# Inverse shuffles 128 to 32 partitions, a last stage of 32-row matmuls, a sine table turned by DMA, and row statistics joined on GpSimd

## The chip, the core and the metric

The kernel runs on one core of a Trainium2 chip. A core has five engines with queues of their own: TensorE (matmuls, in the profile PE, its weight loads PEld), VectorE (DVE), ScalarE (ACT), GpSimd (POOL) and SyncE (SP, which here only issues DMAs). They share 16 DMA engines, an SBUF of 128 partitions, and a PSUM of eight banks that TensorE writes and VectorE and ScalarE read. The metric is the device time of one execution in microseconds. Before the change it is 172.41, the median of three runs (171.73 to 172.89).

## What is computed

Input x is A_q, 2048 rows of 448 columns. Two blocks with residuals follow each other; both start with a layernorm over the columns.

```python
def _A_ref(q, k, v, shift_k, ssm_k, ssm_D):
    # k_shift: causal 4-tap filter of k along the rows, one filter a column
    kv = k_shift * v
    # y: causal convolution of each column of kv with that column of ssm_k (length 2048)
    y = y + kv * ssm_D[None, None, :]
    return q * y

def _B_ref(x, w1, b1, w2, b2):
    h = _layernorm(x, axis=-1)
    u = jnp.einsum("bsd,sf->bdf", h, w1) + b1      # 2048 rows -> 1792
    u = _gelu(u)
    y = jnp.einsum("bdf,fs->bds", u, w2) + b2      # 1792 -> 2048 rows
    return y.transpose(0, 2, 1)

h = x + _A_ref(_layernorm(x), A_k, A_v, A_shift_k, A_ssm_k, A_ssm_D)
h2 = h + _B_ref(_layernorm(h), B_w1, B_b1, B_w2, B_b2)
```

## The kernel before

**Layout.** Row s = 16 q + r lies in partition q, slot r. Every big tile is a view of one SBUF tensor, "arena", so the profile names them all arena; PSUM is "ps".

**The convolution** is a Fourier transform along the 2048 rows, a product, and a transform back, all as matmuls with sine tables that the kernel makes itself (`emit_tables`: integer phases on VectorE at L837 to L844, the sine on ScalarE at L847, in two halves). The steps:

- *kv*: k is transposed on TensorE (L966), filtered by matmuls with diagonal matrices (L992) and multiplied by v on VectorE (L1007). *kT*: the filter ssm_k is transposed (L1038).
- *Stage 1* (`emit_stage1`, tags k1 for the filter and u1 for kv): matmuls with 32 columns of table E (L1059, four at a time in four column groups), evictions of two banks at a time (L1069, for the first k groups L1067 on VectorE), then DMA shuffles within the arena (L1075; per pair of evictions two on GpSimd's queue and one on SyncE's).
- *Stage 2* (`emit_stage2`, k2 and u2): matmuls with the block table FW (L1094), evictions of 128x896 (L738 on ScalarE, L741 on VectorE; with a scale for k at L739 and L742).
- *Inverse stage 1* (`emit_products_i1`, i1): for each index one VectorE product of all four real and imaginary pairs (L1160, 128x1792), then matmuls with the inverse tables MA, MB, MN in two row groups of 64 (L1177), evictions to TU (L738), and shuffles from TU to TZ (L1200; L1189 for the last pair). A shuffle of index j moves 128 partitions of TU into 8 partitions of TZ, 16 pieces each. Rows 14 and 15 have shuffles of their own. The last pair uses re-ordered tables ML, and the first two output rows (NZ = 2) read its share directly from TU through a padded table EW, which small DMAs fill (L1118, L1127).
- *Inverse table*: ET is E transposed on TensorE (`emit_ct`, L1108, 32 transposes) with four copies.
- *Inverse stage 2* (`emit_i2`, i2): for each output row group r, two matmuls over all 128 partitions of TZ (L1299), for r below 2 four more with EW (L1307). Then on each r: a gate (1 + y/std) on ScalarE (L1316) or VectorE (L1318), the product with the centred x on VectorE (L1326; for r below NX = 4 a product straight out of PSUM, L1337), sums for the second layernorm (L1343 and L1346, or L1355 on ScalarE), the power -0.5 on GpSimd (L1379) and the normalised row Q (L1385).

**Row statistics of x** (`emit_q`): per r one bn_stats (L1236) and one bn_aggr (L1238) on VectorE, then an addition and a power on GpSimd (L1244, L1247). For four r, `emit_xn` writes normalised rows ahead of need (L1256 to L1269).

**The MLP** (`emit_mlp`): the first half of W1 (seven blocks of 128 features) accumulates in seven PSUM banks while the rows Q arrive (L1432), with the remaining last-stage matmuls between; then seven blocks with all rows present (L1442), then W2 (L1453), with gelu at L1422 and the output at L1456 and L1464. The weights W1 and W2 come by DMA on SyncE (L1405, L1409, L1416), those of W1 after its first quarter behind the last shuffles.

**What sets the order.** `_Sched` keeps for each engine a queue that is written out by hand: the strings of ORDER name the operations as step:number ("i2.9:0", the first operation of that step). An engine takes its operations in that order, and waits are put in from the data they share and from PSUM banks and ring buffers as they come free. Estimated costs (`est`) settle only which bank or buffer an operation gets and in which order the program is written. Matmuls called "warm" (L1210) and "dummy" (L1025) compute nothing that is used. The issuing of DMAs also has a queue: each engine's DMAs stand in its own order string.

Of the kernel before, what the change touches and what calls it, by code (L numbers as in the profile page):

```python
# [7 lines left out]
ALU = mybir.AluOpType  # L8
# [167 lines left out]
class _Sched:  # L176
# [50 lines left out]
    def op(self, W, fn, r=(), w=(), br=(), bw=(), n=0, kind=None, est=None, dmab=None, keng=16, rate=None, after=(), safter=(), mode=0):  # L227
# [3 lines left out]
        o = _Op()  # L231
# [351 lines left out]
def _build(nc, A_q, A_k, A_v, A_shift_k, A_ssm_k, A_ssm_D, B_w1, B_b1, B_w2, B_b2, out):  # L583
# [8 lines left out]
    R = 16  # L592
# [45 lines left out]
    with ctx:  # L638
# [27 lines left out]
        TU = view(o_TU, [R, 2, D])  # L666
        KN = view(o_KN, [4, S])
        W2 = [view(o, [NFC // 2, S]) for o in o_W2]
        TZ = view(o_TZ, [R, 2, D])
        G = view(o_G, [NFC, D])  # L670
        X = view(o_X, [R, D])
        E = view(o_E, [2 * R, 128], f16)
# [843 lines left out]
```

## Time and profile before

| | |
|---|---|
| median of three runs | 172.41 us |
| profiled execution, span from first to last instruction | 171.2 us |
| TensorE busy | 161.5 us (94%) |
| VectorE busy | 99.1 us (58%) |
| ScalarE busy | 92.9 us (54%) |
| GpSimd busy | 58.1 us (34%) |
| share of the chain of waits: TensorE, ScalarE, DMA | 66%, 14%, 10% |
| MLP: first matmul of L1432, of L1442, of L1453 | 80.95, 104.96, 126.14 us |
| mean granted TensorE clock | 1.00 |

The profile lists no time for the profiled execution apart from its span; the rest to the median, 1.2 us, lies outside the span. Busy times are unions over an engine's instructions; the mean duration of one instruction can be longer than its distance to the next, since neighbours overlap. Start and length columns are microseconds. A DMA row on a queue ("SPq") is the time to issue it; "to landing" counts from the issue to its completion.

### The profile page before, as it was taken

The numbers are of one execution on the slowest core, as the hardware profiler recorded it, in microseconds if no ns is written. First come the engines' busy times: TensorE is split into PE (matmuls) and PEld (weight loads), VectorE is DVE, ScalarE is ACT, GpSimd is POOL, SyncE is SP. The second block draws the span as 40 slices with busy tenths as digits, with TensorE's granted clock in tenths as the row PEclk, the third lists the DMA queues.
The fourth block names the chain that finished last, engine by engine and source line by source line (L and its number), as shares of the span: only waits on it lengthen the run. The fifth ranks groups of instructions, "written<-read, shape, count | busy, mean of one in ns | idle before, by whom it ended". The sixth has DMA issues, their size and how long they took to land.

```text
span 171.2 us, 3572 instructions
## 1 busy us (share of the span) xinstructions
PE 161.5 (94%) x1425; PEld 94.7 (55%) x1425; DVE 99.1 (58%) x187; ACT 92.9 (54%) x133; POOL 58.1 (34%) x150
## 2 busy tenths in 40 slices
PE   6979999979889999988999999999999999999993
PEld 2765845443334434453555555555567777777783
DVE  7988988859899999969988810000003223132232
ACT  3798788988999999999877336321210000000000
POOL 8344827590820573466788820000000000000000
PEclk9999999999999999999999999999999999999999
DMA  5999587675749855667999999960000111101111
GB/s 156 417 315 386 176 257 280 230 301 193 255 120 369 302 173 175 206 182 237 344 342 405 415 419 425 414 279 0 0 0 4 54 54 54 54 4 54 54 54 54
DMA packets 15708, 35.15 MB, mean 205 GB/s; under 512 B 3564, under 2 KB 9980, under 8 KB 15692
## 3 DMA queue, kind: packets, MB, share of 16 engines
q1 hardware_dynamic: 13020, 29.20, 46.9%
q0 software_dynamic: 2528, 5.65, 10.2%
q8 instruction: 11, 0.18, 0.5%
q10 hardware_dynamic: 144, 0.08, 0.2%
q14 instruction: 5, 0.04, 0.1%
HBM read 22.05 MB, written 1.84 MB: 139 GB/s over the span
## 4 chain that ended last, share of the span: by engine, by line
PE 66%; ACT 14%; DMA 10%; DVE 4%; POOL 2%; SPq 2%; issue 1%; DVEq 0%
PE ps L1453 25%; PE ps L1432 12%; PE ps L1442 12%; ACT arena L738 7%; DMA arena<-arena 5%; DMA arena<-in_A_ssm_k_dram 5%; ACT arena L1069 4%; PE ps L1177 4%; PE ps L1094 3%; PE ps L1299 3%; POOL arena L1075 2%; PE ps L992 2%; PE ps L1059 2%; DVE arena L1007 2%; ACT arena L739 1%
## 5 line engine op out<-in xcount | busy, mean ns | idle before, releaser
L1456 DVE SCALAR_TENSOR_TENSOR arena<-ps,arena 128x448 bf16<-128x448 f32 (+2 forms) x17 | 11.2, 657 | 57.3 <-PE ps L1453 57.2
L1453 PE MATMUL ps<-arena 128*128 128x448 bf16 (+2 forms) x238 | 42.7, 342 | 0.0
L1453 PEld LDWEIGHTS ps<-arena 128*128 128x128 bf16 x238 | 33.3, 145 | 9.5
L738 ACT CAST arena<-ps 128x896 bf16<-128x896 f32 x30 | 24.6, 1012 | 0.2 <-PE ps L1094 0.2
L1432 PE MATMUL ps<-arena 128*128 128x448 bf16 x112 | 22.5, 353 | 0.6 <-DVE arena L1385 0.6
L1069 ACT CAST arena<-ps 128x896 bf16<-128x896 f32 x24 | 20.5, 915 | 3.9 <-PE ps L1059 3.8
L1075 POOL DMA_DIRECT2D arena<-arena x32 | 17.6, 554 | 12.2 <-ACT arena L1069 10.2
L1442 PE MATMUL ps<-arena 128*128 128x448 bf16 x112 | 21.3, 352 | 0.0
L1422 ACT ACTIVATE arena<-ps,arena 128x448 bf16<-128x448 f32 x14 | 8.2, 640 | 18.7 <-PE ps L1442 14.5
L1094 PE MATMUL ps<-arena 128*64 128x448 bf16 x128 | 15.2, 359 | 2.5 <-DMA arena<-arena 0.8
L1432 PEld LDWEIGHTS ps<-arena 128*128 128x128 bf16 x112 | 10.9, 98 | 11.1 <-DVE arena L1385 1.3
L1160 DVE TENSOR_TENSOR arena<-arena 128x1792 bf16<-128x1792 bf16 x16 | 16.7, 1086 | 0.3
L1442 PEld LDWEIGHTS ps<-arena 128*128 128x128 bf16 x112 | 11.0, 98 | 10.2
L1059 PE MATMUL ps<-arena 128*32 128x448 bf16 x256 | 15.0, 355 | 0.8 <-DVE arena L1007 0.5
L1177 PE MATMUL ps<-arena 64*128 64x448 bf16 x128 | 14.5, 351 | 0.1
L1094 PEld LDWEIGHTS ps<-arena 128*64 128x64 f16 x128 | 5.8, 108 | 10.9 <-ACT arena L738 2.9
L1200 POOL DMA_DIRECT2D arena<-arena x11 | 6.5, 593 | 15.3 <-ACT arena L738 15.3
L1177 PEld LDWEIGHTS ps<-arena 64*128 64x128 f16 x128 | 6.0, 94 | 8.3 <-ACT arena L738 2.5
L1007 DVE TENSOR_TENSOR arena<-ps,arena 128x512 bf16<-128x512 f32 (+1 forms) x16 | 9.1, 619 | 2.1 <-PE ps L992 1.8
L1355 ACT ACTIVATE arena<-arena 128x448 bf16<-128x448 bf16 x14 | 8.0, 572 | 3.7 <-DVE arena L1326 3.5
L738 ACT COPY arena<-ps 128x1024 bf16<-128x1024 bf16 (+1 forms) x8 | 8.0, 1067 | 3.0 <-PE ps L966 3.0
L1059 PEld LDWEIGHTS ps<-arena 128*32 128x32 f16 x256 | 5.1, 95 | 7.6 <-DVE arena L1007 2.5
(97 smaller groups left out, 192.5 us busy)
## 6 DMA issues: line engine op xcount, KB each, us to landing
arena<-in_B_w_dram SPq DMA_DIRECT2D x8, 896.0 KB, 8.7
arena<-in_B_w_dram SPq DMA_DIRECT2D x2, 2048.0 KB, 17.3
arena<-arena POOLq DMA_DIRECT2D x32, 112.0 KB, 3.2
arena<-arena SPq DMA_DIRECT2D x16, 224.0 KB, 3.2
arena<-in_B_w_dram SPq DMA_DIRECT2D x2, 1536.0 KB, 18.8
arena<-in_A_k_dram SPq DMA_DIRECT2D x4, 448.0 KB, 5.8
arena<-in_A_v_dram SPq DMA_DIRECT2D x4, 448.0 KB, 9.4
arena<-in_A_q_dram SPq DMA_DIRECT2D x4, 448.0 KB, 5.3
```

The costliest lines, as they stand in the source:

```text
L738: return e.copy(out=dst(), in_=src())
L1007: return e.tensor_tensor(out=v, in0=u.rearrange("p t (r d) -> p t r d", d=64), in1=v, op=ALU.mult)
L1059: op("pe", lambda e, W, b=b, r=r, q=q, x=x, c0=c0: e.matmul(PS[32 * q:32 * q + 32, b.slots[x], 0:D], E[:, 2 * r + x, c0:c0 + 32], src[:, r ...
L1069: return e.copy(out=dst, in_=Ppair(b)) if W == "act" else e.tensor_copy(out=dst, in_=Ppair(b))
L1075: shuf[tag].append(op(q_, lambda e, W, g=g, i=i, a=a, nu=nu, jh=jh: e.dma_start(T[a + i:a + i + 4 * nu - 3:4].rearrange("p (j k) c d -> p ...
L1094: op("pe", lambda e, W, b=bs[h], h=h, j=j, c=c, par=par: e.matmul(PS[64 * par:64 * par + 64, b.slots[c], 0:D], FW[:, 64 * c:64 * c + 64], ...
L1160: op("dve", lambda e, W, m=m, i=i: e.tensor_tensor(out=MR(m.slots[0]).rearrange("p (x y) d -> p x y d", x=2), in0=TU[:, i].unsqueeze(2).br ...
L1177: k = op("pe", lambda e, W, b=bs[h], m=ms[h], par=par, t=t, tab=tab, xy=xy, P=P: e.matmul(Pb(b, par), tab[P, :], MR(m.slots[0])[P, xy, :], ...
L1432: op("pe", lambda e, W, r=r, fc=fc, b=bs[fc]: e.matmul(Pb(b), W1A[:, r, 128 * fc:128 * fc + 128], Q[:, r, :], start=(r == 0), stop=(r == R ...
L1442: op("pe", lambda e, W, r=r, fc=fc, b=b: e.matmul(Pb(b), W1B[:, r, 128 * (fc - n0):128 * (fc - n0) + 128], Q[:, r, :], start=(r == 0), sto ...
L1453: op("pe", lambda e, W, r=r, fc=fc, b=b, d0=d0, d1=d1: e.matmul(Pb(b)[:, d0:d1], W2[fc // 7][:, fc % 7, r:S:R], G[:, fc, d0:d1], start=(fc ...
L1456: op("dve", lambda e, W, r=r, b=b, d0=d0, d1=d1: e.scalar_tensor_tensor(out=X[:, r, d0:d1], in0=Pb(b)[:, d0:d1], scalar=bm[:, r:r + 1], in ...
```

## The change

1. **Index order.** Pairs in stage 2 and inverse stage 1 are no longer 2jj and 2jj+1 but `Jof(jj, x) = (jj >> 1) + 8 (jj & 1) + 4 x`; table E is laid out in blocks of four rows, so its phases are computed in two instructions per half.
2. **Shuffles.** Index J goes from 128 partitions of TU to 32 partitions of TZ (every fourth), in one DMA, all on SyncE: 14 of 224 KB, and for the last pair four halves. GpSimd issues none of them; the separate shuffles for rows 14 and 15, the tables ML and the two filling DMAs at L1118 go.
3. **Last stage.** 32-row matmuls at tile positions 0, 32, 64, 96: r = 4k + g uses row group g. Eight of them make one output row (m = 0..3, two halves). For k = 0 the last block (m = 3) is taken from TU through EW, now for four rows, with four matmuls for each half: 152 in all. All sixteen rows stand ahead of the MLP's first matmul in TensorE's order.
4. **Sine table.** ET comes from four DMA transposes on SyncE, each of 128 x 1024 values of E; the TensorE transposes and their copies go. Four DMAs copy rows of ET to EW.
5. **Row statistics.** bn_aggr is gone; for each group of four r, six small operations on GpSimd join the halves of bn_stats and add eps, and a power follows.
6. **A new order** on all five engines, and `est` values given for SyncE's DMAs. The warm matmuls move. In SyncE's order the four transposes stand between the loads of k and v, the EW copies among the stage 1 shuffles; x chunks 1 and 2 stand behind the first inverse shuffle.

```diff
-        if o.is_dma:
+        if o.is_dma and est is None:
             o.est = {e: (585.0 if e == "pool" else 1400.0 if e == "act" else 700.0 if keng <= 8 else 460.0) for e in o.engs}
...
-        TZ = view(o_TZ, [R, 2, D])
+        TZ = view(o_TZ, [4, R // 4, 2 * D])
...
-        E = view(o_E, [2 * R, 128], f16)
-        ET = view(o_ET, [2 * R, 128], f16)
+        E = view(o_E, [R * 256], f16)
+        ET = view(o_ET, [R // 4, 8, 128], f16)
...
+        def Jof(jj, x):
+            return (jj >> 1) + 8 * (jj & 1) + 4 * x
...
+        def emit_et():
+            sch.t0 = T_TH + 1.0
+            for k in (2, 3, 0, 1):
+                op("sp", lambda e, W, k=k: e.dma_start_transpose(out=ET[:, k], in_=E[:, 1024 * k:1024 * k + 1024]),
+                   r=[(o_E + 2048 * k, 2048)], w=[(o_ET + 2048 * k, 2048)], dmab=128 * 2048, est=1350.0, rate=400.0)
...
+            op("pool", lambda e, W: e.memset(EW, 0.0), w=[(o_EW, 2048)], est=950.0)
+            for j in range(4):
+                op("sp", lambda e, W, j=j: e.dma_start(EW[0:128:4, 2 * j:2 * j + 2, :].rearrange("p a b -> p (a b)"),
+                                                       ET[j:128:4, 0, 6:8, :].rearrange("p a b -> p (a b)")),
+                   r=[(o_ET + 1536, 512)], w=[(o_EW + 512 * j, 512)], dmab=32 * 512, est=600.0)
...
+                m = jj >> 1
+                for h0, h1 in ((0, 1), (1, 2)) if jj == R // 2 - 1 else ((0, 2),):
+                    for par in range(2):
+                        J = Jof(jj, par)
+                        p0 = J >> 2
+                        k = op("sp", lambda e, W, J=J, h0=h0, h1=h1, p0=p0, m=m: e.dma_start(
+                            TZ[p0:128:4, m, :, h0 * D:h1 * D], TU[:, J, h0:h1, :].rearrange("p c d -> p (c d)")),
...
-                    op("dve", lambda e, W, bs=bs, r=r: e.bn_aggr(out=qs[:, r, 0:2], in_=bs), r=[(ob, 24)],
-                       w=[(o_qst + 16 * r, 8)], n=6)
...
+                op("pool", lambda e, W, G4=G4: e.tensor_tensor(out=qs[:, G4, 0:2], in0=bst[:, G4, 1:3], in1=bst[:, G4, 4:6],
+                                                               op=ALU.add), est=250.0, r=cb(1, 8) + cb(4, 8), w=cq(0, 8))
...
+            pb = [_Buf(psum) for r in range(R)]
+            for k in range(R // 4):
+                for m in range(4):
+                    for h in range(2):
+                        js = range(4) if k == 0 and m == 3 else range(1)
+                        for j in js:
...
+                            for g in range(4):
+                                r = 4 * k + g
+                                P = slice(32 * g, 32 * g + 32)
+                                if len(js) == 4:
+                                    J = 3 + 4 * j
+                                    lw, mv, rr = EW[P, 2 * j + h, :], TU[P, J, h, :], [(o_EW + 512 * j + 256 * h, 256), (o_TU + (2 * J + h) * DB, DB)]
+                                else:
+                                    lw, mv = ET[P, k, 2 * m + h, :], TZ[P, m, k, h * D:h * D + D]
...
+                                x = op("pe", lambda e, W, b=pb[r], lw=lw, mv=mv, m=m, h=h, j=j, n_=len(js), g=g: e.matmul(
+                                    Pb(b), lw, mv, start=(m == 0 and h == 0), stop=(m == 3 and h == 1 and j == n_ - 1),
+                                    tile_position=(32 * g, 0)),
+                                   r=rr, bw=[pb[r]], n=D, est=47.0, mode=5)
```

SyncE's order, up to the first weights (decoded above in words):

```diff
-        "loads.6:0 loads.8:0 loads.0:0 loads.1:0 loads.2:0 loads.3:0 loads.13:1 loads.14:0-1 loads.10:0 loads.5:0 "
-        "loads.11:0 loads.4:0-2 loads.12:0 loads.7:0 loads.9:0 k1.11:11 k1.9:11 k1.13:11 k1.15:11 u1.1:11 k1.1:11 "
...
+        "loads.6:0 loads.8:0 loads.14:0 loads.0:0 loads.1:0 loads.2:0 loads.3:0 loads.4:2 loads.14:1 loads.4:1 "
+        "loads.10:0 loads.5:0 et.0:3 loads.13:1 loads.12:0 loads.4:0 et.0:2 et.0:0 loads.9:0 et.0:1 loads.7:0 k1.9:11 "
+        "loads.11:0 ew.0:4 k1.11:11 k1.5:11 k1.15:11 k1.7:11 u1.1:11 k1.13:11 ew.0:3 k1.1:11 k1.3:11 u1.5:11 u1.9:11 "
+        "u1.3:11 u1.7:11 u1.11:11 u1.13:11 u1.15:11 ew.0:2 xload.0:0 xload.3:0 ew.0:1 w1a.0:0 i1.1:20 xload.1:0 "
+        "xload.2:0 i1.1:19 i1.9:19 i1.5:19-20 i1.3:20 i1.3:19 i1.9:20 i1.11:19-20 i1.7:19-20 i1.13:20 i1.13:19 "
+        "i1.15:19-20 i1.15:22 i1.15:21 w1a.1:0 w1a.2:0 w1a.3:0 w1b.0:0-3 w2.0:0-3 mlp.25:15 mlp.27:15 mlp.29:15 "
```

In it, loads.0 to 3 are ssm_k, loads.4 the short filter's weights, loads.5, 6, 8 and 10 chunks of k, loads.7, 9, 11 and 12 chunks of v (rows 0-3, 4-7, 8-11, 12-15 of each partition), loads.13:1 the vector D, loads.14 the biases, and et.0 the transposes.

More of the change, by code (lines that the diff above doesn't have):

```diff
@@ L684, in _build @@
         FW, MA, MB, MN = [view(o_BD + 256 * k, [128], f16) for k in range(4)]
-        NZ = 2
         o_EW = o_I2 + 128
-        EW = view(o_EW, [4 * NZ, 128], f16)
-        o_ML = o_EW + 1024 * NZ
-        ML = [view(o_ML + 256 * k, [128], f16) for k in range(3)]
-        assert o_ML + 768 <= o_TU
+        EW = view(o_EW, [8, 128], f16)
+        assert o_EW + 2048 <= o_TU
         o_GR = (o_WR, o_WR + 8 * DB, o_X, o_X + 8 * DB)
@@ L1158, in emit_products_i1 @@
                     ru = (o_TU + i * 2 * DB, 2 * DB)
-                    aft = [x for w in wbufs for x in w.readers] if i == 0 else [mfirst[0]]
+                    aft = [x for w in wbufs for x in w.readers] if not mfirst else [mfirst[0]]
                     op("dve", lambda e, W, m=m, i=i: e.tensor_tensor(
@@ L1196, in emit_products_i1 @@
[L1196 to L1204 removed]
+                    evac(lambda J0=J0, h=h: TU[:, J0:J0 + 5:4, h, :], lambda b=bs[h]: Ppair(b),
+                         [(o_TU + (2 * J0 + h) * DB, DB), (o_TU + (2 * J0 + 8 + h) * DB, DB)], bs[h], 2 * D)
@@ L1213, in _build @@
         mfirst = []
-        o_bst = small(4 * 24)
+        o_bst = small(R * 24)
+        o_qd = small(R * 4)
         o_qst = small(16 * 16)
@@ L1242, in emit_q @@
[L1242 to L1249 removed]
+                    op("dve", lambda e, W, r=r: e.bn_stats(out=bst[:, r], in_=X[:, r, :]), r=[(o_X + r * DB, DB)],
+                       w=[(o_bst + 24 * r, 24)], n=D, kind="1x")
@@ new lines, in emit_q @@
+                if g % 2 == 0:
+                    continue
+                r0 = 2 * g - 2
+                G4 = slice(r0, r0 + 4)
+                cb = lambda c, nb: [(o_bst + 24 * (r0 + i) + 4 * c, nb) for i in range(4)]
+                cq = lambda c, nb: [(o_qst + 16 * (r0 + i) + 4 * c, nb) for i in range(4)]
+                cd = [(o_qd + 4 * r0, 16)]
+                op("pool", lambda e, W, G4=G4: e.tensor_tensor(out=qs[:, G4, 0:2], in0=bst[:, G4, 1:3], in1=bst[:, G4, 4:6],
+                                                               op=ALU.add), est=250.0, r=cb(1, 8) + cb(4, 8), w=cq(0, 8))
@@ L1293, in emit_i2 @@
                     r = r0 + i
[L1294 to L1310 removed]
+                    sch.t0 = T_I2 + 1.0 + T_DI2 * r
+                    b = pb[r]
+                    oA = o_TZ + (4 * (r % 4) + r // 4) * 2 * DB
+                    A = view(oA, [D], f32)
+                    tz = [(oA, 2 * DB)]
                     sch.t0 += 0.01
```

208 lines of the change are left out of this document (65 added, 143 removed), and 135 rows, old and new, of the table ORDER.

## The prediction

> **What bounds the kernel now.** I read the chain of waits first, for the places where the end of the work is decided; then a table of the busy time by stretch, cut at the joints of that chain; then the rows of the groups for prices. The chain, from the last inverse eviction on (start us, length us, what):
>
> ```profile
> 69.59 1.12 ACT arena L738
> 70.72 1.25 ACT arena L1269 x2
> 71.96 0.81 ACT arena L738
> 72.77 0.29 issue
> 73.06 2.14 DMA arena<-arena
> 75.20 0.53 PE ps L1299 x2
> ...
> 80.58 0.32 DVE arena L1385
> 80.90 0.05 issue
> 80.95 1.31 PE ps L1432 x6
> ...
> 104.96 21.19 PE ps L1442 x112
> 126.14 42.09 PE ps L1453 x231
> ```
>
> After 104.96 TensorE runs without a gap; I leave that part alone. From 80.95 to 104.96 TensorE is full too: 112 matmuls of the first MLP half at about 0.189 us (21.2) and 14 left over from the last inverse stage (L1299, 7 x 0.38 = 2.7). What can change lies ahead of 104.96, at three joints: 72.77 (end of the last inverse eviction; call it T), 75.19 (the last shuffle has landed, L1299 starts), 80.95 (first normalised row, MLP starts).
>
> ```profile
> core 0: us, PE busy (x) PEld busy (x) DVE busy (x) ACT busy (x) POOL busy (x), PEclk, DMA share, GB/s
> 5.47:44.00 38.53, 35.61 (x644) 21.10 (x641) 32.53 (x49) 33.48 (x38) 20.62 (x37) 1.00 0.78 275
> 44.00:47.94 3.94, 3.31 (x30) 1.38 (x32) 3.88 (x5) 3.46 (x5) 3.52 (x7) 1.00 0.96 303
> 47.94:72.77 24.83, 23.95 (x209) 10.18 (x206) 24.50 (x38) 24.83 (x32) 8.99 (x17) 1.00 0.68 222
> 72.77:80.95 8.18, 6.86 (x52) 3.77 (x49) 6.77 (x23) 7.80 (x12) 5.47 (x10) 1.00 0.67 204
> ```
>
> From 47.94 to T ScalarE is busy 24.83 of 24.83 us: its queue of evictions sets T. VectorE (24.50) follows closely. Ahead of 47.94 ScalarE idles 5.5 of 42.5 us and VectorE 6.1; nothing is full there except, in parts, the DMA engines (share 0.78 to 0.96).
>
> **The change, part by part.**
>
> *Work on ScalarE up to T.* Prices are start to start: 28 evictions of line 738 run from 47.94 to 70.71, 0.81 each; a k2 eviction (L739) 0.84 (four in 3.35); a transpose copy about 0.95; two normalised rows (L1269) 1.57. Counting the two orders: one copy of the k transposes less (-0.95), one k2 eviction less (-0.84), one u2 eviction more (+0.81), the two L1269 rows now behind the last eviction (-1.57). Sum -2.55. VectorE up to T: copy +0.65 and k2 eviction +1.05, u2 eviction -1.06, the first table copy -0.69, eight aggregations at about 0.12 -1.0: sum -1.0. Both engines are nearly full, so T moves by something between the two unless idle time changes: -2.55 to -1.0. I take -1.3, near VectorE's end, because what ScalarE loses partly goes to VectorE.
>
> *SyncE's early queue.* A bias load moved ahead of the four kernel loads delays them by its issue, 0.46 (the b row took 0.46 there), and the fourth of them heads the chain at 11.48: up to +0.45, inside the lower end above. Four DMA transposes (256 KB each) and four EW copies are new in this queue. The first transpose waits for the first half of the sine table, about 7.7 by the before's VectorE and ScalarE rows (2.1 + 3.5 of phases + 2.0 of sine). Queued behind it: D, three of four v loads, the short-filter weights. The diff's planner books 1.35 us per transpose; no row shows one. Between a plain issue (0.43) and twice the planner's figure, the load of v rows 0-3 goes out at 12 to 20 instead of 10; with the planner's figure at about 15. Landing then takes 3.2 us (SBUF shuffles of this queue) to 9.7 (the v loads before): 18 to 25. Its reader was the product at 19.39, and the new order puts four more k1 steps (4 x 0.85 = 3.4) ahead of it, so it is wanted at about 22.8. Mostly hidden; I take 0, ends 0 and +2.
>
> *Bandwidth of the transposes.* They move 1.05 MB inside a stretch where DMA shares are 0.8 to 0.9. At 417 GB/s (the second of the page's 40 slices) that is 2.5 us of all engines, and spare share up to 30 us is about 5 us: hidden. If they go in 256-byte pieces, 4,096 pieces at 38 ns (queue q10: 0.2% of 16 engines' span over 144 packets) to 99 ns (q1) would be 10 to 25 us. I take the low end, since the rows they read are 2 KB, like most of the packets shown; the high end is a rival. The Trainium skill ("DMA: Bandwidth & Descriptors", Latency and other measured facts) gives 261 GB/s for a DMA transpose, 350 to 400 when contiguous: by it, an estimate of 4.0 or 2.8 us, hidden as well. No run so far shows it.
>
> The wait of the first EW copy for its transpose stands in SyncE's queue ahead of k1's and u1's shuffles. SyncE spent 18.8 us of that stretch waiting for evictions (its own waits, L1075), so 1 or 2 us there are covered; without that cover they would pass to u1's shuffles and to T.
>
> *Shuffles.*
>
> ```profile
> L1200 SPq DMA_DIRECT2D arena<-arena x17: 666/668/684, 60.8 to 83.1; - x17
> L1200 POOL DMA_DIRECT2D arena<-arena x11: 542/594/677, 57.2 to 71.6; - x11
> DMA to landing us min/median/max: 3.0/4.2/6.3
> ```
>
> Before: 12 on GpSimd, 20 on SyncE. After: 18 on SyncE, 18 x 0.67 = 12.1 us inside a 25 us stretch, so the queue keeps up, except at the end, where the last four go out one after another. Two follow the first half's eviction (0.81 ahead of T), two the last: last issue starts at about T + 1.2, landing 2.9 later (L1189): T + 4.1, against T + 2.4 before. That is 1.7 us worse. But the first group of outputs (r 0-3) takes its last block straight from TU through EW, so it needs no landing: 4 rows are ready about T + 0.6.
>
> *Last stage.* 152 matmuls of 32 rows. One at a time they would cost 152 x 0.189 = 28.7 us; four at once 7.2, beside 40 x 0.189 = 7.6 before. The nearest rows: column tiles of 32 (L1059, 24 in 1.32 us, 0.055 each), row tiles of 64 (L1177, 16 in 1.73, 0.108 each, two at once). I take 0.055, so 8.4; about 24 run before T, and the 8 blocks after the landing of each of three groups are 1.3 us. The transposes of the sine table (32, 2.0 us of TensorE) and their four copies go; they lay beside the DMA wait, worth nothing but VectorE's 0.69 above.
>
> *From T to the MLP.* VectorE's new order, start to start: four products 2.5, two statistics with their joins 1.4, two gates 1.2 (they cover GpSimd's power), small step 0.1, gate of r 11 0.6, row 0 0.35: 6.2, from T + 0.6: T + 6.8. The other lock is PSUM: the MLP's first four banks come free with the gates of r 8-11, and ScalarE does five gates (0.61 to 0.72) from about T + 4.5: T + 7.6 to 8.1. I take T + 7.6, before T + 8.18. From there VectorE feeds rows: row 2 at +2.9 and row 4 at +5.9 behind row 0 where TensorE wants them at 2.66 and 5.3: stalls of 0.6 to 1.9, I take 1.4. No matmul of the last stage is left inside. End of the first half: 7.6 + 21.2 + 1.4 = T + 30.2; before 104.96 - 72.77 = 32.2. So -2.0; ends -3.4 (6.8 + 21.2 + 0.8) and 0 (8.5 + 21.2 + 2.5).
>
> *Statistics.* 28 small GpSimd operations at 0.24 and four powers replace ten; +4 us on GpSimd, which loses 12 issues (7.1 us): hidden, 0. Weight loads go out earlier (SyncE spent 75.0 to 83.8 on leftover shuffles); the MLP did not wait for them: 0.
>
> **Sum.** -1.3 + 0 - 2.0 = -3.3 against the profiled span of 171.2, which gives 167.9. The median of the three runs is 172.41, 1.2 above that span (start and end outside it), so 169.1. Its own ends: -2.55 - 3.4 gives 166.5; +0.45 + 2 (queue, v) - 1.0 + 0 gives 173.9 if everything goes badly, more likely 172.
>
> **Rivals.**
> 1. *Slower: the transposes fill the DMA engines.* Place: the loads and k1 shuffles between 8 and 25 us. Price: 10 us of fabric in place of 2.5, less 5 of spare share, is +5 on T; with the -3.3 kept, 174.1, at the top of the price far more. It decides from about 8 us of engine time for the four. For it: no such row exists, share 0.87 from 10 to 20 us. Against: 2 KB rows. Chance 0.18, time 174 to 178.
> 2. *The order gives it back.* The gates wait for the later landing (T + 4.1), banks and rows come late, the idle time ahead of 47.94 grows by 1 to 2: about 172. For it: 1.7 us later landing, one queue. Against: r 0-3 don't need it. Chance 0.14.
> 3. *TensorE slows after a pause.* The warm matmuls (L1210) move away from the place ahead of the MLP. Row: the nine first dummies (L1025) start 0.37 us apart after an idle engine, 0.189 later on, though the clock column says 1.00 in both. Price: nine at 0.18 more, 1.6 us: 170.7. It needs a pause of some microseconds before the MLP; the last stage's matmuls leave about 1. Chance 0.06. The Trainium skill ("TensorE: Matmul & The Clock Gate", HAM oscillation) sets the limit at about 3.4 us of idle time; by that rule the pause I expect is too short.
> 4. *The tiles don't overlap.* At 0.108 each the last stage takes 16.4 us and the MLP starts some 5 us later: 174. For it: neighbours in the new order sometimes share a row group. Against: L1059. Chance 0.03.
>
> **Numbers.** Forecast 169.1 with chance 0.59, its own range 166.5 to 172. The range to hold it 8 times in 10, with rival 2 and the near side of 1: 166.4 to 174.6. One per cent (1.7 us) is about what these runs tell apart from no change. Faster by more than that (under 170.7): 0.58, most of the forecast and half of rival 3; within: 0.2; slower (over 174.1): 0.22, rivals 1 and 4 in the main.
>
> **What would show it.** T at about 71.5, with ScalarE full from u2's first eviction; the MLP's first matmul 7 to 8 us behind T and not sooner than row 0 on VectorE; no last-stage matmul inside the first half; that half 22 to 23 us long. Transposes landing within 3 us of their turn and no wait of VectorE's v products on a load. I am wrong if T lies later than 73, if the first MLP half shows over 2.5 us of gaps, or if the 152 matmuls take over 12 us of TensorE.

## The result and the profile after

| | before | after |
|---|---|---|
| median, us | 172.65 (171.73 to 173.63, 4 runs) | 179.81 (179.07 to 180.78, 4 runs) |
| span of the profiled execution, us | 171.2 | 177.3 |
| first u2 eviction starts | 47.94 | 53.90 |
| last inverse eviction ends | 73.57 | 79.41 |
| MLP's first matmul | 80.95 | 88.77 |
| first half of the MLP ends | 104.96 | 110.84 |

The change is slower: ratio 1.042, interval [1.036, 1.048]. The forecast was 169.1 with a range of 166.4 to 174.6: sign and range were both missed. The ratios here and below leave out executions over 1.5 per cent above the fastest of their kernel; each of those shows a mean granted clock of 0.99 or less.

One correction first. The prediction called 72.77 the end of the last inverse eviction. That is the end of a link in the chain of waits; ScalarE's own row (two casts from 71.71, 1.86 long) ends at 73.57. After has no such link, so from here on T is the end of ScalarE's last cast, 73.57 before and 79.41 after, and "u2" as a time is the start of the first u2 eviction. ScalarE's rows, two of before, then two of after:

```profile
47.94 22.77 ACT L738 CAST arena<-ps 128x896 bf16<-128x896 f32 x28 [0.23 <-PE ps L1094]
71.71 1.86 ACT L738 CAST arena<-ps 128x896 bf16<-128x896 f32 x2
53.90 23.61 ACT L750 CAST arena<-ps 128x896 bf16<-128x896 f32 x29 [0.74 <-PE ps L1109]
77.69 1.72 ACT L750 CAST arena<-ps 128x896 bf16<-128x896 f32 x2 [0.18 <-PE ps L1158]
```

The three stretches are: up to u2 47.94 before, 53.90 after (+5.96); u2 to T 25.63 and 25.51 (-0.12); T to the end of the first MLP half 31.39 and 31.43 (+0.04). What follows takes 66.2 and 66.5. The whole loss lies ahead of u2, and the gain expected behind it is not there.

Busy time by stretch after (engines with instruction counts, clock, DMA share, GB/s), cut at the new joints:

```profile
core 0: us, PE busy (x) PEld busy (x) DVE busy (x) ACT busy (x) POOL busy (x), PEclk, DMA share, GB/s
5.47:50.00 44.53, 38.29 (x655) 21.75 (x654) 35.65 (x59) 32.41 (x37) 23.21 (x46) 0.96 0.94 266
50.00:53.90 3.90, 2.87 (x29) 1.45 (x29) 3.48 (x4) 2.90 (x5) 1.45 (x3) 1.00 0.95 275
53.90:79.41 25.51, 24.98 (x218) 9.74 (x217) 24.98 (x34) 25.33 (x32) 7.36 (x17) 1.00 0.65 229
```

From u2 to T ScalarE is full as before. Ahead of 53.90 it idles 13.1 of 48.4 us (5.5 of 42.5 before), and the granted clock up to 50.00 is 0.96. The chain of waits shows where:

```profile
17.80 0.56 SPq L1121
...
18.41 0.58 SPq L916
...
19.03 1.24 SPq L1121
...
20.32 6.48 DMA arena<-in_A_v_dram
...
27.50 1.62 DVE arena L1022 x3
...
29.16 2.43 PE ps L1074 x24
```

L1121 is the DMA transpose, L916 a v load, L1022 VectorE's product with v, L1074 the stage 1 matmul. Transposes on SyncE's queue stand on the critical chain, ahead of the load of v rows 0-3 (20.32), which lands 6.48 later. The queue itself in order of time:

```profile
7.86 2.75 SPq L1121 DMA_TRANSPOSE arena<-arena  x1
...
12.21 6.15 SPq L1121 DMA_TRANSPOSE arena<-arena  x2
18.41 0.58 SPq L916 DMA_DIRECT2D arena<-in_A_v_dram  x1
19.03 1.24 SPq L1121 DMA_TRANSPOSE arena<-arena  x1
20.32 0.58 SPq L916 DMA_DIRECT2D arena<-in_A_v_dram  x1
```

The four transposes hold SyncE's queue for 10.1 us (2.75 + 6.15 + 1.24); the loads issued between them hold it for 0.4 to 0.6 each. The line's own view (least, median, longest issue in ns; then landing), the group of the v products and the packets:

```profile
L1121 SPq DMA_TRANSPOSE arena<-arena x4: 1237/2785/3282, 7.9 to 19.0; - x4
DMA to landing us min/median/max: 4.7/6.7/7.9
```

```profile
DMA packets 20365, 36.25 MB, mean 205 GB/s; under 512 B 7340, under 2 KB 15036, under 8 KB 20348
...
L1022 DVE TENSOR_TENSOR arena<-ps,arena 128x512 bf16<-128x512 f32 (+1 forms) x16 | 8.8, 617 | 5.1 <-DMA arena<-in_A_v_dram 4.5
```

Packets under 512 bytes were 3,564 before: 3,776 more, about what 1.05 MB in 256-byte pieces makes (4,096). VectorE waits 4.5 us for v. That wait has a second price. TensorE stood still for 2.37 us up to 27.96 (and 1.44 up to 21.98), and then the granted clock fell (clock, DMA share and GB/s are the last three numbers of each row):

```profile
26.00:28.00 2.00, 0.04 (x4) 0.04 (x8) 1.11 (x3) 0.00 (x0) 1.99 (x4) 1.00 1.00 322
28.00:30.00 2.00, 1.92 (x28) 0.66 (x32) 2.00 (x4) 1.34 (x2) 0.00 (x0) 0.65 1.00 283
30.00:32.00 2.00, 2.00 (x28) 0.73 (x22) 2.00 (x3) 0.65 (x2) 1.01 (x2) 0.50 0.89 351
```

The 24 matmuls of L1074 at 29.16 took 2.43 us; 24 of this kind took 1.32 in the prediction's row. Such a stretch, with a granted clock near 0.5, is called half rate below.

Behind T, TensorE's timeline (start, length, idle time before in brackets):

```profile
78.31 3.40 PE L1287 MATMUL ps<-arena 32*128 32x448 bf16 x59
81.64 0.36 PE L1181 MATMUL ps<-arena 128*128 128x448 f16 x1
81.94 0.36 PE L1287 MATMUL ps<-arena 32*128 32x448 bf16 x1
82.23 0.36 PE L1181 MATMUL ps<-arena 128*128 128x448 f16 x1
82.53 1.49 PE L1287 MATMUL ps<-arena 32*128 32x448 bf16 x21
83.95 0.36 PE L1181 MATMUL ps<-arena 128*128 128x448 f16 x1
84.37 2.08 PE L1287 MATMUL ps<-arena 32*128 32x448 bf16 x38
86.50 0.36 PE L1181 MATMUL ps<-arena 128*128 128x448 f16 x1
86.80 2.04 PE L1287 MATMUL ps<-arena 32*128 32x448 bf16 x32
```

L1287 is the last stage, L1181 a warm matmul. The 32-row tiles do overlap, 59 in 3.40 us (0.058 each), but only some 18 of them fit ahead of T, TensorE is taken until the MLP starts, and four warm matmuls stand among them.

### The profile page after: what moved, and what is told of

Its sections match the earlier page's. It is cut to its first block, busy times and chain, and to the rows that moved or that the text cites. A ratio compares the mean times of both kernels' runs of the same rounds, so it can differ in the third digit from the quotient of the medians.

```text
span 177.3 us, 3704 instructions
## 1 busy us (share of the span) xinstructions
PE 165.0 (93%) x1505; PEld 94.2 (53%) x1505; DVE 99.7 (56%) x176; ACT 87.3 (49%) x126; POOL 56.1 (32%) x149
## 4 chain that ended last, share of the span: by engine, by line
PE 62%; DMA 13%; ACT 11%; SPq 4%; DVE 3%; POOL 3%; issue 2%; DVEq 0%; POOLq 0%
PE ps L1440 24%; PE ps L1429 12%; PE ps L1419 8%; PE ps L1158 6%; DMA arena<-in_A_ssm_k_dram 5%; DMA arena<-arena 4%; PE ps L1287 4%; ACT arena L750 4%; DMA arena<-in_A_v_dram 4%; ACT arena L1084 3%; PE ps L1109 3%; PE ps L1074 2%; ACT arena L1307 2%; PE ps L1181 2%; ACT arena L751 1%
## 5 line engine op out<-in xcount | busy, mean ns | idle before, releaser
L1084 ACT CAST arena<-ps 128x896 bf16<-128x896 f32 x24 | 20.6, 910 | 10.6 <-PE ps L1074 10.5
L750 ACT CAST arena<-ps 128x896 bf16<-128x896 f32 x31 | 25.3, 992 | 0.9 <-PE ps L1109 0.7
L1419 PE MATMUL ps<-arena 128*128 128x448 bf16 x112 | 21.7, 353 | 0.4 <-DVE arena L1376 0.3
L1429 PE MATMUL ps<-arena 128*128 128x448 bf16 x112 | 21.5, 353 | 0.0
L1090 POOL DMA_DIRECT2D arena<-arena x32 | 17.8, 561 | 11.4 <-ACT arena L1084 10.1
L1074 PE MATMUL ps<-arena 128*32 128x448 bf16 x256 | 16.5, 379 | 4.5 <-DVE arena L1022 2.4
L1429 PEld LDWEIGHTS ps<-arena 128*128 128x128 bf16 x112 | 10.9, 98 | 10.5 <-ACT arena L1409 0.4
L1158 PE MATMUL ps<-arena 64*128 64x448 bf16 x128 | 15.1, 351 | 0.3
L1074 PEld LDWEIGHTS ps<-arena 128*32 128x32 f16 x256 | 5.1, 97 | 13.0 <-ACT arena L1084 3.9
L1022 DVE TENSOR_TENSOR arena<-ps,arena 128x512 bf16<-128x512 f32 (+1 forms) x16 | 8.8, 617 | 5.1 <-DMA arena<-in_A_v_dram 4.5
L1287 PE MATMUL ps<-arena 32*128 32x448 bf16 x152 | 9.7, 349 | 0.1
L1208 DVE BATCH_NORM_STATS2 arena<-arena 128x6 f32<-128x448 bf16 x16 | 9.3, 615 | 0.0
```

What stands on the lines that cost most here:

```text
L750: return e.copy(out=dst(), in_=src())
L1074: op("pe", lambda e, W, b=b, r=r, q=q, x=x, c0=c0: e.matmul(PS[32 * q:32 * q + 32, b.slots[x], 0:D], E[:, c0:c0 + 32], src[:, r, :], start ...
L1084: return e.copy(out=dst, in_=Ppair(b)) if W == "act" else e.tensor_copy(out=dst, in_=Ppair(b))
L1090: shuf[tag].append(op(q_, lambda e, W, g=g, i=i, a=a, nu=nu, jh=jh: e.dma_start(T[a + i:a + i + 4 * nu - 3:4].rearrange("p (j k) c d -> p ...
L1158: k = op("pe", lambda e, W, b=bs[h], m=ms[h], par=par, t=t, tab=tab, xy=xy, P=P: e.matmul(Pb(b, par), tab[P, :], MR(m.slots[0])[P, xy, :], ...
L1287: x = op("pe", lambda e, W, b=pb[r], lw=lw, mv=mv, m=m, h=h, j=j, n_=len(js), g=g: e.matmul(Pb(b), lw, mv, start=(m == 0 and h == 0), stop ...
```

## The experiments

Theory at the start: the transposes hold SyncE's queue, what stands behind them (v loads, shuffles) comes late, and that is all of the loss. Rivals: their small pieces load the DMA engines for everybody; the new order costs something by itself; the last stage's order wastes its gain. Each ratio below is to runs of the kernel before on the same chip. "Front" is what lies ahead of u2, "tail" what lies between T and the end of the first MLP half. Of the order strings only the stretch that changes is shown, with neighbouring operations of one step drawn together.

### Where the transposes stand

*e1*: the transposes and EW copies moved back in SyncE's order, two behind its last u1 shuffle, two behind two x loads.

```diff
-loads.5:0 et.0:3 loads.13:1 loads.12:0 loads.4:0 et.0:2 et.0:0 loads.9:0 et.0:1 loads.7:0
+loads.5:0 loads.13:1 loads.12:0 loads.4:0 loads.9:0 loads.7:0
...
+u1.15:11 et.0:2 et.0:3 xload.0:0 xload.3:0 et.0:0 et.0:1
```

> The changed kernel with its four DMA transposes moved in SyncE's order from between the loads of k and v to behind the last u1 shuffle (two ahead of the x loads, two behind the first two), and the four EW copies behind the first three inverse shuffles; nothing else moves. Queue theory (the transposes hold SyncE's queue, so that the v loads go out 9 to 10 us late) and bandwidth theory (their packets fill the DMA engines while k and v load) both expect the front to come back: the first eviction of u2 near 48 instead of 53.9, 172 to 174 us. If the loss sits in the new order or in the last stage, 178 to 180.

*e2*: D, the filter weights and all v loads ahead of the first transpose.

```diff
+loads.5:0 loads.13:1 loads.12:0 loads.4:0 loads.9:0 loads.7:0 loads.11:0 et.0:3 et.0:2 et.0:0 et.0:1
```

> The changed kernel with D, the last short-filter weights and all four v loads ahead of the first transpose in SyncE's order; the transposes stay in the front, ahead of the first k1 shuffle of that queue. Queue theory: the v loads go out by 10 us, the 4.5 us wait of VectorE's product for v is gone; the transposes now hold SyncE's k1 shuffles for up to 8 us, which have some 13 us of slack: 173 to 176. Bandwidth theory: the engines are as full between 8 and 22 us as before, v still lands late, 178 or more.

*e3*: a plain DMA of the same 256 KB in place of each transpose (the table is copied, not turned).

```diff
-e.dma_start_transpose(out=ET[:, k], in_=E[:, 1024 * k:1024 * k + 1024])
+e.dma_start(ET[:, k].rearrange("p a b -> p (a b)"), E[:, 1024 * k:1024 * k + 1024])
```

> The changed kernel with each DMA transpose replaced by a plain DMA of the same 256 KB from E to ET at the same place of the queue (the table is copied, not turned, so the last stage multiplies by other numbers). If turning is what holds the queue and fills the engines, an issue takes about 0.5 us, the v loads for rows 0-3 go out near 14 instead of 20 (the third copy still waits for the second half of the sine table at 12), and the time falls to 173 to 175. If any 1 MB in this place costs it, 178 to 180.

*e4*: the kernel before plus four such transposes at like places of its SyncE order, into space that is overwritten later.

```diff
+op("sp", lambda e, W, k=k: e.dma_start_transpose(out=EV[:, k], in_=EF[:, 1024 * k:1024 * k + 1024]), ...
```

> The kernel before, with four DMA transposes of the same size added at the corresponding places of SyncE's order, into the space of ET, which the kernel's own transposes overwrite later. Queue or bandwidth theory: 177 to 180, five to seven more than before, with VectorE's product waiting for v. If the new order alone makes the loss, 172 to 174.

Measured:

| | ratio to before | u2 | T |
|---|---|---|---|
| after | 1.042 [1.036, 1.048] | 53.90 | 79.41 |
| e1, late | 1.016 [1.011, 1.021] | 51.56 | 77.89 |
| e2, v first | 1.016 [1.007, 1.025] | 51.95 | 77.42 |
| e3, plain copies | 1.012 [1.001, 1.023] | 50.39 | 75.87 |
| e4, before + transposes | 1.063 [1.053, 1.072] | 59.81 | 85.44 |

So the place costs 2.6 of the 4.2 per cent: with the v loads out first, the wait for v is gone, though the transposes still hold the queue from 10.92 for 12.49 us in e2. In e4 the old order wants v even sooner: its products wait 7.32 and 3.66 us for v loads, and TensorE then runs at half rate (clock 0.50 from 28 to 36 us), so its loss is larger than the 177 to 180 us expected. But 1.2 to 1.6 per cent stay, whatever is done with the transposes, and u2 near 48, as hoped for in e1, was not reached. The profiled execution of e1 has a half-rate stretch of its own early on (0.79, then 0.50, from 14 to 18 us), so its u2 and T are later than the ratio says.

### The rest: traffic, or the new order

*e5*: no turning at all; the last stage and EW read E.

```diff
+        o_ET = o_E
         ET = view(o_ET, [R // 4, 8, 128], f16)
...
-... ("et", emit_et, ()), ...
```

> The changed kernel with no turning of the sine table at all: the four transposes are left out and the last stage and the EW copies read the unturned table E itself (so the values of the last stage are others). If the four transposes are the whole loss, u2's first eviction starts near 48 us, T near 73, and the time is that of before within 1% (ratio 0.99 to 1.005). If the new order loses something by itself, u2 starts at 49.5 to 50.5, T is 75 to 76, the MLP still starts at T + 9.4, and the ratio to before stays at 1.007 to 1.012, like with plain copies in place of the transposes (1.012).

*e8*: e5, with b1 behind the four ssm_k loads again, v rows 12-15 and 0-3 behind D, and EW copies behind the first inverse shuffles.

```diff
+loads.6:0 loads.8:0 loads.0:0 loads.1:0 loads.2:0 loads.3:0 loads.4:2 loads.14:0 loads.14:1 loads.4:1
+loads.10:0 loads.5:0 loads.13:1 loads.12:0 loads.4:0 loads.7:0 loads.9:0 loads.11:0 k1.9:11
```

> As the kernel without the turn, and in SyncE's order the b1 load stands behind the four filter loads again, the v rows 12-15 and 0-3 right behind D, and the EW copies behind the first inverse shuffles. If the front's loss is SyncE's order, the first k1 eviction starts about 1 us sooner (15.2 to 15.5) and u2 starts 1 to 2 us sooner than without this edit. If it is the order of the matmuls and products (first kv products wanted at 22.3 instead of 18.3, last u1 shuffles late), u2 starts within 0.5 us of the kernel without this edit, and the wait for the u1 shuffles (4 to 5 us of the chain) stays.

*e9*: e5, with all five engines' orders up to u2 as before the change (k2 steps renamed to the new index order).

```diff
-k1.15:0-7 k1.4:0-7 k1.5:0-7 kv.10:0-23 kv.11:0-27 kv.9:0-27 k1.6:0-7 k1.7:0-7 k1.0:0-7
+k1.14:0-7 kv.9:0-27 k1.15:0-7 k1.4:0-7 kv.11:0-27 u1.0:0-7 u1.1:0-7 k1.0:0-7 k1.1:0-7
```

> The changed kernel without the turn (the last stage reads the unturned table E, so its values are others), and all five engines' orders up to the first u2 matmul as in the kernel before, with the k2 steps renamed to the new index order; from u2 on the changed kernel's own order. If the new front order is the rest of the front's loss (ScalarE waited 1.25 us three times for u1 matmuls that stand behind bunches of filter matmuls, and 1 us for the first k1 matmuls), u2's first eviction starts at 47.7 to 48.5 instead of 50.9, T is 73.2 to 74, the time 172.5 to 173.3 and the ratio to before 0.995 to 1.005. If instead the new index order (k2, u2) or the traffic itself costs, u2 starts no sooner than 50 and the ratio stays above 1.01.

Measured: e5 1.018 [1.013, 1.022], u2 at 50.93, both above what was expected if the new order loses something (1.012, 50.5); e8 1.009 [1.004, 1.013]; e9 1.003 [0.998, 1.008], u2 at 48.07, T at 73.57, end of the first MLP half at 105.00. e5 also says more of e2: with the transposes behind the v loads the time is that without any (1.016 and 1.018), so in the changed order the wait for v is their whole price, as far as intervals of about one per cent can tell, and their traffic costs nothing there. e8's profile shows a half-rate stretch early on that e5's lacks, so its joints (u2 51.41) can't be set beside e5's; its ratio says that SyncE's front order, the three moves of e8 together, is about half of this part. e9 settles the sum: without the turn and with the old front order, these three joints are those of the kernel before within 0.13 us, and the time is the same. ScalarE's row of e9:

```profile
48.07 23.60 ACT L833 CAST arena<-ps 128x896 bf16<-128x896 f32 x29 [0.57 <-PE ps L1192]
```

All other parts of the change together, with no turn to pay for at all, come to +0.3 per cent (-0.2 to +0.8): no gain.

What the rest of the new order does is seen in TensorE's timeline of e5 (L1008 filter matmuls, L1075 stage 1):

```profile
22.79 2.62 PE L1008 MATMUL ps<-arena 64*128 64x256 bf16 x80
25.34 1.42 PE L1075 MATMUL ps<-arena 128*32 128x448 bf16 x24
27.03 0.94 PE L1075 MATMUL ps<-arena 128*32 128x448 bf16 x16 [0.28 <-ACT arena L1085]
27.91 1.73 PE L1008 MATMUL ps<-arena 64*128 64x256 bf16 x52
29.57 0.56 PE L1075 MATMUL ps<-arena 128*32 128x448 bf16 x8
30.06 1.73 PE L1008 MATMUL ps<-arena 64*128 64x256 bf16 x52
```

and of e9 (L1090, L1157):

```profile
21.98 1.06 PE L1090 MATMUL ps<-arena 64*128 64x256 bf16 x28
22.97 1.32 PE L1157 MATMUL ps<-arena 128*32 128x448 bf16 x24
24.57 1.43 PE L1157 MATMUL ps<-arena 128*32 128x448 bf16 x24 [0.27 <-DVE arena L1105]
25.93 1.06 PE L1090 MATMUL ps<-arena 64*128 64x256 bf16 x28
```

In this stretch nearly all of ScalarE's work comes from stage 1. The new order runs four k1 steps early and then filters in blocks of 80 and 52 matmuls (2.62 and 1.73 us); the old one filters in blocks of 24 or 28 (0.84 or 1.06) between stage 1 steps from 20 us on. ScalarE's waits of 12 to 52 us, by what it waited for: e5

```profile
ACT arena L1085 <- PE ps L1075: 6.6, 5, 2.4
```

and e9

```profile
ACT arena L1167 <- PE ps L1157: 3.2, 7, 1.2
```

No run moved these blocks alone: that they are the other half is an inference from the two rows.

### What the transposes' price is made of

*e11*: the whole change, with the old front order and the four transposes behind the last v load.

```diff
+loads.12:0 loads.7:0 loads.9:0 et.0:3 et.0:2 et.0:0 et.0:1 k1.11:11 k1.9:11 k1.13:11 k1.15:11
```

> The whole computation: the changed kernel with the order up to u2 of the kernel before, and the four DMA transposes directly behind the last v load in SyncE's queue. If the transposes cost only what stands behind them, they now hold back SyncE's third of the k1 shuffles alone: the first of these goes out at about 23.5 instead of 19.3 us, all of them are due only at k2 (35 us), u2's first eviction starts at 48.0 to 48.6 and the ratio to before is that of the run without a turn (1.003; 0.998 to 1.008). If their 4,096 pieces or the turning itself load the DMA engines for everybody, k1's shuffles land late, k2 starts 1.5 to 4 us later and the ratio is 1.012 to 1.03.

Measured: 1.024 [1.021, 1.027], u2 at 51.89. The expectation that these shuffles are due only at k2 was wrong. VectorE's timeline in e11 (L1165: a k1 eviction that also adds D):

```profile
28.86 2.09 DVE L1165 TENSOR_TENSOR arena<-ps,arena 128x896 bf16<-128x896 f32 x2 [4.68 <-DMA arena<-arena]
```

The eviction waits until a buffer of the stage 1 ring has been shuffled out, and SyncE's share of those shuffles stands behind the transposes. To tell that from their traffic:

*e13*: e9, and SyncE's shuffle of k1.15 (whose eviction ends late) first, so that the others are held as long with no byte more to move.

```diff
-k1.11:11 k1.9:11 k1.13:11 k1.15:11
+k1.15:11 k1.11:11 k1.9:11 k1.13:11
```

> As the kernel with the old front order and without a turn (ratio 1.003), and SyncE's shuffle of k1.15, whose eviction ends only at about 22.7 us, stands first among its shuffles: the others go out from about 23.3 us on instead of 19.2, as behind the four transposes, but not a byte is moved more. If the transposes' price is the hold of SyncE's queue, VectorE's first k1 product after 24.4 us waits 3.5 to 4.7 us for a landing (the eviction buffers are freed by those shuffles), u2's first eviction starts at 51 to 52 and the ratio is 1.018 to 1.026, as with the transposes there (1.024). If it is their 4,096 pieces on the DMA engines, u2 starts at 48 to 49 and the ratio stays below 1.008.

Measured: 1.022 [1.016, 1.028]. The same wait in e13:

```profile
27.69 2.09 DVE L1165 TENSOR_TENSOR arena<-ps,arena 128x896 bf16<-128x896 f32 x2 [3.53 <-DMA arena<-arena]
```

The hold alone gives a loss of the same size. The profiled execution is the fastest of its five (174.72 against a median of 177.08), and its u2, 49.57, is sooner than expected (51 to 52) and only 1.5 us behind e9's; so the row shows the mechanism, and the ratio its size. Two more executions, at a mean clock of 1.00, took 176.38 and 177.08, so the ratio doesn't come from half rate; what else they waited for no trace shows. The price belongs to the old front order: in e2 the queue is held as long, but VectorE waits only 1.7 us for a shuffle, and the time is e5's.

*e14*: the whole change, old front order, two transposes behind SyncE's last u1 shuffle and two behind the second inverse shuffle; with the tail edit of e12 below.

```diff
+u1.15:11 et.0:2 et.0:3 xload.0:0 xload.3:0 w1a.0:0 i1.1:20 xload.1:0 xload.2:0 i1.1:19 et.0:0 et.0:1 i1.9:19
```

> The whole computation: old front order up to u2, two transposes behind SyncE's last u1 shuffle and two behind the second inverse shuffle, the EW copies after those; the last block of rows 4 to 7 ahead of rows 8 to 11, the four warm matmuls of the tail ahead of u2.8. If the transposes cost nothing where nothing due stands behind them, u2 starts at 48.0 to 48.6, the MLP at T + 8.5, and the ratio to before is 0.993 to 1.003. If they still delay the x loads and the inverse shuffles (each held SyncE's queue for 2.4 to 2.8 us), VectorE's inverse products or the statistics wait, T - u2 grows from 25.5 to 27 or more, and the ratio is 1.005 to 1.02.

Measured: 1.013 [1.005, 1.020]; u2 at 47.99 as hoped, but T - u2 is 29.5. Here it is the traffic. SyncE's queue and VectorE's inverse products in e14:

```profile
44.76 4.39 SPq L1204 DMA_TRANSPOSE arena<-arena  x2
```

```profile
48.03 1.09 DVE L836 CAST arena<-ps 128x896 bf16<-128x896 f32 x1
52.37 2.22 DVE L1227 TENSOR_TENSOR arena<-arena 128x1792 bf16<-128x1792 bf16 x2 [3.25 <-DMA arena<-arena]
```

The last u1 shuffles (GpSimd, 46.0) were issued beside two transposes and landed 6.3 us later; in e9 such shuffles took 3.4 in the median, 4.1 at most, and the first inverse product started at 49.16. TensorE idled 1.25 and 0.97 us in this wait and then ran at half rate (0.67 and 0.50 from 54 to 58 us), which is in the 4 us as well. So e14 trades the hold for shuffles that land late. In e1 the first inverse product waits 0.97 us in the same way, but its ratio, 1.016, is not above e5's.

### The tail, and the turn on TensorE

*e6*: e5, with the last block of rows 4 to 7 (i2.21, i2.22) ahead of all of rows 8 to 11 in TensorE's order.

```diff
+i2.19:0-3 i2.20:0-3 i2.21:0-3 i2.22:0-3 warm.12:0 i2.23:0-3 i2.24:0-3
```

> As the kernel without the turn, and in TensorE's order the last block of rows 4 to 7 (8 matmuls) now stands ahead of all blocks of rows 8 to 11. If that place in the order is what holds the gates, the first gate starts right after the last shuffle has landed, at about T + 4.2 instead of T + 6.3, the MLP starts at T + 7.5 instead of T + 9.4, and the time is 1.5 to 2 us less than without this edit. Rival: the statistics on GpSimd (the power of rows 4 to 7 ended at T + 3.9, of rows 8 to 11 at T + 5.2) or VectorE's rows take over; then the MLP starts no sooner than T + 8.7, or its first half grows by what was gained, and the time falls by less than 0.7 us.

*e7*: e6 and e8's front, with the sine table turned on TensorE (32 transposes, four copies).

```diff
+e.transpose(out=Pbf(b, 0, f16)[:, 128 * i:128 * i + 128], in_=E[:, 1024 * k + 128 * i:1024 * k + 128 * i + 128], identity=IH)
```

> The whole change with these edits: the sine table is turned on TensorE (two groups of eight transposes ahead of k2, two ahead of u2, where TensorE waits for shuffles) with two copies on ScalarE and two on VectorE, TensorE's last-stage order and SyncE's front order as in the two runs beside it. If the shuffle waits cover the turn, u2 starts within 0.5 us of the run without a turn and with this front order, and the time is the sum of the two edits' gains: 171.5 to 173 us, not slower than before. If they don't cover it, u2 starts 1 to 2 us later (16 transposes of 0.06 to 0.1 and two copies of 0.95 on ScalarE) and the time is 173.5 to 175.

*e10*: the turn on TensorE in e9's front (one copy on ScalarE, three on VectorE), e6's tail, and the four warm matmuls of the tail moved ahead of u2.8.

```diff
+et.0:0-7 et.1:0-7 k2.0:0-3 k2.1:0-3 k2.2:0-3 k2.3:0-3 et.2:0-7 k2.4:0-3 k2.5:0-3
...
+u1.15:0-7 et.3:0-7 k2.8:0-3
...
-i2.13:3 warm.11:0 i2.14:3 warm.1:0
+i2.13:3 i2.14:3
```

> The whole computation: the changed kernel with the order up to u2 of the kernel before, the sine table turned on TensorE (32 transposes) with three copies on VectorE and one on ScalarE at their idle places around k2, the last block of rows 4 to 7 ahead of rows 8 to 11, and the four warm matmuls of the tail moved ahead of u2.8. If the copies fit into VectorE's idle time (1.11, 0.82 and 0.66 us there before), u2 starts within 0.7 us of the run beside it; the MLP starts at T + 8.3 to 8.8 instead of T + 9.4 (0.5 from the block's place, 0.3 for each pair of warm matmuls on TensorE's way to the gates); the time is 171.8 to 173, ratio 0.99 to 1.0. Rival: the copies delay k2 by 1 us or more and eat the tail's gain: ratio 1.0 to 1.01.

*e12*: e11 with e10's tail (e6's line and the last two lines above).

> As the run beside it, and the tail's order: the last block of rows 4 to 7 ahead of all blocks of rows 8 to 11, and the four warm matmuls of the tail moved ahead of u2.8. If the tail's matmul order is worth what it gave with the TensorE turn, the MLP starts at T + 8.5 instead of T + 9.4, its first half ends at T + 30.5 to 30.7 instead of T + 31.3, and the time is 0.7 to 0.9 us less than beside it (ratio to before 0.994 to 1.003 if that one is at 1.003). Rival: the landing of the last shuffle (T + 4.7 there) now sets the gates; then the gain is under 0.4 us.

| | ratio to before | u2 | T | MLP starts | first half ends |
|---|---|---|---|---|---|
| after | 1.042 | 53.90 | 79.41 | T + 9.4 | T + 31.43 |
| e5, e9, e11 (tail as after) | 1.018, 1.003, 1.024 | 50.93, 48.07, 51.89 | 76.42, 73.57, 77.38 | T + 9.4 (e5, e9) | T + 31.43 each |
| e6 | 1.016 [1.011, 1.021] | 53.34 | 78.81 | T + 8.9 | T + 30.9 |
| e7 | 1.016 [1.010, 1.021] | 50.29 | 75.78 | T + 9.1 | T + 31.1 |
| e10 | 1.009 [1.004, 1.013] | 49.19 | 74.85 | T + 8.5 | T + 30.7 |
| e12 | 1.019 [1.013, 1.025] | 54.73 | 80.40 | T + 8.5 | T + 30.5 |

The block's place alone gives 0.3 to 0.5 us of the first half's end, with the warm matmuls moved as well 0.7 to 0.9: closer to the rival named for e6 than to the 1.5 to 2 hoped for. The u2 and T of e6 and e12 can't be set beside e5's and e11's, for their profiles ran at half rate ahead of u2 (e6 from 14 to 18 us, e12 from 30 to 38); the distances from T can. What is late next is the last shuffle, as TensorE's timeline of e10 shows:

```profile
73.77 4.18 PE L1376 MATMUL ps<-arena 32*128 32x448 bf16 x79
79.56 3.84 PE L1376 MATMUL ps<-arena 32*128 32x448 bf16 x72 [1.61 <-DMA arena<-arena]
```

The copies of the turn weren't hidden: u2 starts 1.1 us later in e10 than in e9, and e7 lies at 1.016 where e8 lies at 1.009. No version that computes the whole beat the kernel before; the nearest is e10. A turn hidden entirely would bring e10's tail to about 0.998 of before by these numbers (1.003 less 0.7 to 0.9 us); that wasn't tried, and intervals as wide as these could not tell it from no change.

## Why the prediction was wrong

1. *SyncE's early queue* ("I take 0, ends 0 and +2") is the step that failed first. The 1.35 us booked for an issue came from a planner, and I let it decide between bounds that were 8 us apart (v out at 12 to 20). The issues took 1.24 to 3.28; v rows 0-3 went out at 20.32, the late end of those bounds, and landed at 26.8 where 22.8 was wanted. After against e5: u2 3.0 us later, the half rate behind the wait included; 4.2 against 1.8 per cent. And the step looked only at the loads behind the transposes. e11 and e13 show that in the old front order SyncE's share of the stage 1 shuffles is nearly as costly to hold (2.1 and 1.9 per cent over e9), because the ring of eviction buffers waits for it; in the new order (e2) no price of that hold is seen.
2. *The new order* had a term only where it moved work (four k1 steps in front of v, the b row), and was otherwise in the rival "the order gives it back", idle time growing by 1 to 2. It measured 2.9 us (e5 against e9) and is the second failed step. The b row's term, "up to +0.45", was too small as well: the last filter load landed at 12.56 in place of 11.48 (13.08 in e5, 11.37 in e9), and moving the b row back is one of e8's three moves. What the prediction took as cover for a late v was probably part of the cost: k1 steps run ahead leave ScalarE without evictions while TensorE filters.
3. *Bandwidth of the transposes*: 2.5 us of all engines was mis-sized. They add 4,224 packets and, by the shares of the hardware queue q1 below (e9, then e11), 53.0% of 175.2 less 49.4% of 171.4 = 8.2 us. The 256-byte pieces that I put at the high end are what happened, at 31 ns each (8.2 x 16 / 4,224). The reason for the low end, rows of 2 KB "like most of the packets shown", misread the page: 9,980 of the 15,708 packets before are under 2 KB. In the front the hold outweighs the pieces (e2, e13), beside the last u1 shuffles they show (e14).

```profile
q1 hardware_dynamic: 14444, 31.21, 49.4%
```

```profile
q1 hardware_dynamic: 18668, 32.26, 53.0%
```

The Trainium skill ("Advanced Engine Details and Errata", X-Bar Transpose (TRN2)) has transposes as fast as regular DMAs. Here plain copies of the same bytes added 2.8 us (e3 against e5: 51.4% of 173.7 less 49.6% of 174.3), the transposes 7.0 (e2 against e5) to 8.2: the measurement decides. From issue to landing the two don't differ that way: 6.9 to 8.5 us for the plain copies of e3, 4.7 to 7.9 for the transposes after.

4. *Work on ScalarE up to T*, -1.3: -0.1 from u2 to T, nothing ahead of it. The copy and the k2 eviction taken off ScalarE (1.8 of the 2.55) lay ahead of u2, where it idles 5.0 us in e9 too; that u2 starts at 48.07 there says they were worth nothing. In the full stretch one more cast and a wait of 0.18 ate most of what the two normalised rows had left behind.
5. *From T to the first half's end*, -2.0: 0.0. The price of a tile was right (0.058 for 0.055), the last landing too (about T + 3.5 for T + 4.1), the first half too (22.07 long, 0.9 of it stalls, for 22.6). Wrong was "ready about T + 0.6": row 0's product starts at 81.18, T + 1.8, since only about 18 matmuls ran before T. Then TensorE, not the list of VectorE's work, leads to the gates: ScalarE's first gate starts at 85.72, T + 6.3, where I had T + 4.5, behind a block that stands late in TensorE's order and warm matmuls of 0.3 each. e6, e7, e10 and e12 give back 0.3 to 0.9 of it. On the T of this section the MLP's start went from T + 7.4 to T + 9.4; the gain of 2.0 that it then has over before is the last-stage matmuls no longer inside the first half.
6. *Statistics*, 0: not isolated. e9 bounds them with all else.
7. Of the rivals, the first had the sign and the pieces, but the wrong price: the queue, not full engines, decided. The third, a slower TensorE after a pause, was placed ahead of the MLP; it came behind the wait for v, where 24 matmuls cost 1.1 us more, and in e8 after far shorter pauses than the rival asked for (last section). The tiles overlapped, which rules out the fourth.

## What to carry to other kernels

An issue of an unmeasured kind on a queue is to be priced by what stands behind it until the next slack, shuffles that free ring buffers included; a planner's figure is no row. That slack belongs to the order around it: the same hold cost 2 per cent in one order and nothing in the other. Work that feeds the bottleneck engine is better kept interleaved with work that doesn't: with the feeding steps run ahead, ScalarE's waits for them were 6.6 us in place of 3.2. Where a change has several parts, the run with the old order and the new algorithm (e9) tells at once which of them the time belongs to.

## What the runs showed of the hardware

- A 256 KB DMA transpose within SBUF held SyncE's queue 1.24 to 5.14 us (e2 the longest) and landed 3.5 to 10.9 us after its issue; plain copies of that size in its place were issued in 0.47 to 0.62 us.
- TensorE ran at half rate after pauses of 2.37 us, with 1.44 shortly before (after, clock 0.65 and 0.50 for some 4 us), and 2.68 us (e11, 0.67 and 0.50), but also after two waits of 0.64 and 0.69 us (e8, 0.50 from 13.5 to 16.5 us). A pause of 1.82 us (e2) and one of 1.61 (e10) were not followed by it. So the length of one pause doesn't decide it, and what does these runs don't show. The Trainium skill ("TensorE: Matmul & The Clock Gate", HAM oscillation) names gaps over about 3.4 us; here less was enough, and the prediction's use of that limit was too sure.
